# A state-space convolution and a gated feed-forward layer: the first part's tasks in another order, and both early inverse units behind the last spectral product

## The chip, the cores and the metric

One core of one Trainium2 chip. TensorE (PE) does the matmuls, VectorE (DVE), ScalarE (ACT) and GpSimd (POOL) the elementwise work, and SyncE (SP) issues nearly all transfers. The metric is the device time of one execution in microseconds, the median of several runs.

## The reference

`x` is one sequence of 2048 tokens with 640 channels; `mod` gives shifts, scales and gates from a small vector `c`.

```python
h = layernorm(x) * (1 + ca) + sa
K = 2.0 * real(einsum("dn,dnl->dl", C, exp(A * dt * pos)))       # one filter of 2048 taps for each channel
y = irfft(rfft(h, 2 * L) * rfft(K, 2 * L), 2 * L)[:L]            # a causal convolution
x = x + ga * (y + h * D_skip)
h = layernorm(x) * (1 + cb) + sb
x = x + gb * ((silu(h @ w1) * (h @ w3)) @ w2)                    # 640 -> 1728 -> 640
```

## The kernel before

The kernel has two parts. The **first part** (up to about 390 us) does the convolution through a Fourier transform written as matmuls, in five channel blocks `b` = 0 to 4 of 128 channels. The **second part** is the feed-forward layer, token block by token block; the change doesn't touch its code.

The first part is cut into 1532 *tasks*. Each is added to a plan with a name, an engine (or a choice of engines) and the tasks that it must follow. `Plan.run` then issues them in a fixed order, a list of numbers `ORDER` at the head of the file; a letter behind a number (a, d, p) picks ACT, DVE or POOL where a task may run on several. The class `InOrder` ties every instruction of an engine behind the one issued before it on that engine, so `ORDER` is at once the order of work on each engine. What an instruction needs from other engines it waits for; what stands behind it on its own engine waits too. For block `b`:

- `g{b}.{c}`, c = 0 to 7: the filter's generator, 16 channels at a time. `ph` and `z0` to `z2` on POOL (phases, magnitudes), `s0` to `s4` on ACT (sines), `m0` to `m4` on DVE (products), `p` on PE (`kps`), `r` on ACT and `d` on DVE (rows of the filter, `ks`). Ahead of them stand the tables `t{b}` and the exponentials (`al8{b}`, `exp{b}`, `mag{b}`; `al8` and `mag` on POOL or DVE).
- `h{b}.{i}`: the normalized input; `n` on ACT or DVE, `x` and `a` on DVE, stored by `o`, fetched back transposed by `h{b}.f`.
- `hh{b}.{i}` and `k{b}.{i}`, eight each: first transform stage of the input and of the filter. `m` on PE (`ps`), `e` the eviction to `sp` on ACT or DVE.
- `w{b}.{i}`, eight: second stage and spectral product. `f` on PE (`fh`) and `h` on ACT (`hq`) for the input, `k` on PE (`fk`) for the filter, `x0`, `x1`, `c` on DVE (`fp`, `fk`, `fp`). `k` needs all eight `k{b}.e`.
- `z{b}.{j}`, four: inverse of the second stage. `z` on PE (`fz`, two banks; `z{b}.{j}` takes the products w 2j and 2j + 1), `v0`, `v1` the copies to SBUF on ACT or DVE (`zt`, three buffers in turn; the last one `ztl`), `o0`, `o1` the stores on SP.

When the generator of block 4 is done, `change` closes its buffers, opens the buffers of the next part in their place, and issues on SP the loads of the first tokens (`low<-in_x`, four) and of a table (`low<-in_t_wd`). `fx` is a task without an instruction that stands for these loads in the plan. `fw0` and `fw1` load the first two weight tiles of the feed-forward layer (`wr`, `w2r`), `fa0`, `fa1` round them on ACT (`wh`, two instructions, and `w2h`), `fs0`, `fs1` take the rest on POOL. `change`'s x loads and `fw` are held until PE has done what was last issued to it at that place of the order (`behind`).

The last stage of the inverse for the first 512 tokens comes in two **units**, `ir0` and `ir1`: PE multiplies what `iz0` and `iz1` have read back for channel blocks 0 to 3 (`iy`, two banks in each unit), DVE adds it to x (`low`) and takes four statistics (`bn_stats`) for each of its two rows. The remaining channel block 4 comes after the plan: SP and ACT read back the stores of `z4`, PE passes the time with dummy matmuls (`awake`, 8 and later 3, kept so that PE's clock stays up), and the same `inverse` runs on four rows (L555). Then follow the layer norm, the transposes (`tp`) and the first matmuls of the feed-forward layer (`gu`).

In PSUM the tasks share four banks of one size: three of the tag `f`, taken in turn, and one of tag `x`; of four requests through `pbank` the third takes `x`. `ir` takes `f` banks. Further weight loads of the second part stand behind the plan in the program, but are not tied to its order on SP and lie between its transfers.

Of the kernel before, what the change touches and what calls it, by code (L numbers as in the profile page):

```python
# [34 lines left out]
10 29 25 39 153 35 26 13 62 154 60 155 47 72 74 70 76 66 89 27 48 5 93 87 91 98 49 36 100 33 95 50 94 34 51 32 88 37 52 38  # L35
152p 40 92 156d 53 96 157 90 9 158 6 54 102 159 167 104 55 170 99 11 171 168 97 56 103 184 176 172 57 105 178 173 169 58 188
185 111 177 107 186 67 193 101 122 187 68 189 174 194 160 195 190 64 179 175 123 191 180 109 161 163d 65 181 192 201 113 318
114 115 110 197 182 112 183 303 117 202 340 205 118 108 203 210 341a 106 162 211 124 308 196 204 127 116 138 198 218 313 206
119 128 207 199 130 212 221 129 125 208 134 164 131 165 135 132 209 219 166 222 133 235 140 139 63 214 126 309a 200 220 75 73
77 69 71 213 342 427 228 343a 215 136 223 319a 236 142 141 224 430p 431 229 137 239 428 310 216 429 217 311 227 312 344 304a  # L40
238 244 225 305 237 240 230 345a 424p 241 144 245 143 306 242 320 307 226 432 247 425 252 433 321 231 322 314d 232 255 246 315
253 243 426d 254 256 248 269 233 262 257 249 261 258 234 316 346 272 250 263 259 317 251 270 347a 264 348 260 146 271 145 273
265 274 278 286 275 279 266 280 276 349d 323 287 267 281 277 290 288 268 282 291 350 295 289 292 283 296 441 297 293 147 351d
284 294 285 298 352 148 458 299 445 149 0 582 698d 446 300 447 442 353d 592 324 699 443 450 328 325d 461 583d 336 459 460 329d
577 584 334 444 451 337a 585 301 972p 335a 700d 586 326 462 452 302 330 434 578d 327a 331a 354 448 467 593a 332 437p 579 438
468 439 580 333a 435 856 594 338 355a 453 449 436 358 463 581 595 851 464 475 440 364 454 469 465 455 339d 596 466 470 356 456
476 479 457 362 471 357 477 484 480 472 363 359 492 481 485 360 473 482 365 495 496 361 366 478 379 487 493 380 486 494 367
483 501 497 373 701 488 852a 375 502 857d 489 374 509 498 381 853 587 490 858 499 510 854 513 1399 859 390 704p 504 705 706
391 860 503 855 511 491 474 518 500 376 514 702 505 515 526 377 506 382 378 507 512 383 588a 407 519 527 384 520 528 408 385
861 589 516 703 508 530 590 517 521 591 368 529 707 388a 386a 522 389 543 531 387 536 523 532 537 1400d 369a 392 544 597 524  # L50
862a 545 525 393 1140 535 546 371a 394 533 1401 398 547 372 395 534 1402 1130 560 539 396 553 413 552 397 538 708 414 1403 370
399 540 548 863 564 400 549 561 864 565 554 709 865 598 541 566 569 710 542 401 550 599d 608 1131a 562 555 602 563 570 609a
1132 711p 606 973 712 571 713 604 1133 603d 714 1134 612 607d 1141d 600 601d 866 605a 974p 1142 567 610 613d 1246p 1404 1143
409 611d 551 572 670 568 1144 715 410 867a 636 573 411 574 732 556 719 1135 637 868 557 575 412 671 736 869 630 718 558 1405d
870 720 664 716 721 653 726 717 631 1409 1406 665 647 733 654 725 1407 871 648 734 741 1136a 415 681 724 735 1408 742 616 559
416 737 1414 1137 617a 743 738 417 682 1138 739 418 1139 687 722 744 1410a 620 727 880 723 1411 1125 688 728 749 881a 618 1412
740 576 1413 1415d 621a 729 766 753 876 619a 754 745 1126a 872 1416 750 1417 746 752 873d 1418 877a 1127 624 770 767 760 755
614 1128 768 625a 775 1129 628 615a 758 751 776 626 629a 769 759 622 627d 771 975 882 756 623d 772 761 402 883a 777 773 976
978d 730 778 979 419 774 980 403a 779 747 977 404 757 405d 632 420a 731 748 406 762 783 981 421 649 633 634 780 650 800 787
638 635 781 788 782 651 422a 763 639 789 423 652 655 784 764 640 790 884 656 801 641 878 885a 802 657 792 874 879a 785 658 765  # L60
786 875a 793 642 795 804 803 794 886 645a 643d 791 646 666 810 644 887a 817 1145 796 805 910 667 806 811 797 911 809 921 668
807 820 669 821 938 818 922 812 808 904 819 798 813 822 672 799 905 826 834 823 827 814 673 939 927 828 824 835 674 815 659
825 829 982 928 838 675 839 662d 676 660a 830 663 836 840 661 816 843 983 844 841 944 679d 837 842 831 846 680 945 985p 1247
683 986 677d 987 845 678 689 984 684 847 894 989 685 988 892 690 686 848 691 895a 990 832 893d 896 849 992 993 692 897d 693
991 1248d 994 850 1006 999 995 1000 961 696d 694a 955 998 1009 697 996 695 833 962 890 1001 1007 997 1160 1010 1002 1008 956
1015 1011 1150 1161d 1023 1012 1017 1003 1016 1151a 1013 891d 1146 1024 1027 1018 1014 1156 1025 1147a 1019 1028 1148 1026
1032 1157a 1033 1029 1020 1040 1149d 1034 1030 902 1031 1035 888 1041 1044 1036 1152 1043 889a 1049 1045 898 903d 1042 1046
1051 900 1249 1153a 1050 1047 899d 1158 901a 1052 1048 906 1159a 1057 1053 1004 912 907 1021 1005 1022 908 1037 1252p 913 1061
1250 1054 909 1062 1058 1038 914 1063 923 1039 915 1060 1055 1154 1066 1064 1059 1056 924 916 1419 1155a 1068 1251 925 1067
1074 926 917a 1065 1069 918 940 919a 1075 1078 920 1070 1184 1079 941 1077 1071 1083 1080 942 1076 1178 1185 1085 1081 1091  # L70
943 1212 1179 1084 1072 946 1213 1073 1086 1082 1092 1195 1095 947 1096 929 1094 1087 1196 948 1097 1088 1093 930 949 1218
1098 1108 1102 1089 950 931 1219 1101 1109 932 1100 953a 1111 933 951a 1090 954 1103 1099 1110 952 1112 1104 1201 1253 934a
1117 1254 1113 935 1118 957 1202 1255 1256 1119 1114 963 958 936a 959 1105 1115 937 964 1263 1116 1164 960 1106 1121 1162
1165a 1120 1266 1267 1172 1163a 965 1264 1268 1122 1107 966 1173a 1269 1265 1272 967 1274 1123 1280 1270 1273 1124 1275 1271
1176 970a 1283 1170 968d 1284 971 1177d 1285 969 1174 1281 1276 1286 1291 1168 1282 1175a 1289 1287 1235 1259d 1297 1290 1169a
1171d 1277 1236 1292 1288 1166 1260 1301 1298 1293 1302 1229 1167d 1278 1300 1303 1306 1294 1279 1299 1230 1308 1424 1304 1314
1307 1295 1180 1425a 1296 1309 1305 1420 1181 1317 1318 1310 1197 1319 1315 1182 1421a 1434 1320 1198 1316 1183 1311 1321 1199
# [107 lines left out]
class K:  # L185
# [866 lines left out]
    def run(self):  # L1052
# [46 lines left out]
        b = NB - 1  # L1099
# [13 lines left out]
        add = plan.add  # L1113
# [5 lines left out]
        z = {}  # L1119
        W = self.W["tail"]  # L1120
# [649 lines left out]
```

## Time and profile before

| | |
|---|---|
| median of 3 runs | 971.52 us (971.05 to 973.86) |
| profiled execution | 970.77 us |
| its span, first to last instruction | 968.8 us |
| mean granted TensorE clock | 0.966 |
| busy in the span: PE, DVE, ACT, POOL | 860.8, 712.9, 517.0, 336.1 us |
| moved by DMA | 113.18 MB |

A row of the timeline reads: start in us, duration in us, engine, line, operation, what is written from what, shape of output and input, how many instructions are merged; in brackets the engine's idle time before it and what ended it. A row of the groups ends with the total busy time and the mean of one instruction in ns, then the idle time ahead of them. A row of the windows has the stretch, its length, and for each engine the busy time and the number of instructions, then PE's granted clock, the share of the DMA engines and GB/s. In the page's strips each digit is the busy share of a fortieth of the span in tenths. L146 is the line of `InOrder`, through which all of the first part is issued.

### The profile page before, as it was taken

To read this page: it belongs to the slowest core of one execution; us is meant where nothing else is said; L and a number is where in the kernel's file an instruction comes from. 1 tells how busy PE (TensorE), PEld (TensorE's weight loads), DVE (VectorE), ACT (ScalarE), POOL (GpSimd) and SP (SyncE) were. 2 spreads that over 40 slices of the span, in tenths; PEclk is the share of its full clock that TensorE was granted. 3 is DMA by queue.
4 is the path that set the end of the run, shared out by engine and by line. 5 is a ranking of instruction groups with operands and counts; after the bars stand their busy time and mean duration, and the time that the engine had idled before them with its cause. 6 is when DMAs were issued, how large, how long until landed. Compare 5 with 4: busy or idle time off the path is not lost.

```text
span 968.8 us, 20106 instructions
## 1 busy us (share of the span) xinstructions
PE 860.8 (89%) x8017; PEld 685.6 (71%) x8017; DVE 712.9 (74%) x1292; ACT 517.0 (53%) x874; POOL 336.1 (35%) x345
## 2 busy tenths in 40 slices
PE   2165767899999997899999999999999999999997
PEld 1033655787878773667778888888888888888875
DVE  7888999999999973657684365566467777765763
ACT  5878879979888830523143243345234444445331
POOL 2789998599999530100000000000213223300000
PEclk9585989999999998999999999999999999999999
DMA  9956526624140296987523353223131122122242
GB/s 241 236 175 213 119 59 169 161 68 111 37 99 25 72 276 184 233 203 189 136 82 91 100 148 111 82 82 109 28 82 55 55 54 55 42 82 90 85 152 82
DMA packets 122821, 113.18 MB, mean 117 GB/s; under 512 B 11752, under 2 KB 106472, under 8 KB 121320
## 3 DMA queue, kind: packets, MB, share of 16 engines
q1 hardware_dynamic: 121992, 110.99, 42.6%
q8 instruction: 63, 1.03, 0.5%
q10 hardware_dynamic: 736, 0.92, 0.3%
q14 instruction: 30, 0.25, 0.1%
HBM read 90.91 MB, written 20.97 MB: 115 GB/s over the span
## 4 chain that ended last, share of the span: by engine, by line
PE 66%; DVE 13%; DMA 7%; ACT 6%; issue 3%; POOL 3%; SPq 1%; DVEq 0%; ACTq 0%; POOLq 0%
PE acc L1024 17%; PE p L777 16%; PE gu L987 6%; PE gu L989 6%; PE gu L988 6%; DVE yy L146 3%; DMA xs<-in_x 3%; PE ps L146 2%; PE kps L146 2%; DVE fp L146 2%; ACT tr L146 2%; PE fz L146 2%; DVE xx L146 2%; PE iy L555 2%; DMA sp<-in_w_mod 1%
## 5 line engine op out<-in xcount | busy, mean ns | idle before, releaser
L987 PE MATMUL gu<-xh,wh 128*128 128x512 f32 x270 | 105.0, 394 | 0.9 <-ACT xh L569 0.7
L989 PE MATMUL gu<-xh,wl 128*128 128x512 f32 x270 | 105.4, 390 | 0.0
L988 PE MATMUL gu<-xl,wh 128*128 128x512 f32 x270 | 105.3, 390 | 0.0
L777 PE MATMUL p<-x,wch 128*128 128x512 f32 x312 | 92.7, 390 | 0.0
L796 POOL TENSOR_TENSOR ws<-wp 128x256 f32<-128x256 f32 x13 | 9.6, 739 | 229.8 <-DVE wcl L570 114.9
L146 POOL TENSOR_TENSOR yy<-e,e 128x512 f32<-128x512 f32 x80 | 87.1, 1103 | 3.0 <-PE kps L146 2.3
L146 POOL TENSOR_TENSOR ph<-p,p 128x1024 int32<-128x1024 int32 x40 | 78.5, 1964 | 16.1 <-ACT tr L146 15.7
L146 DVE TENSOR_TENSOR yy<-yy,tr 128x512 f32<-128x512 f32 (+1 forms) x80 | 75.1, 944 | 5.0 <-POOL yy L146 4.6
L681 ACT ACTIVATE wh<-wr 128x640 fp32r<-128x640 f32 x51 | 34.9, 731 | 63.3 <-PE gu L988 54.1
L146 PE MATMUL kps<-yy,xx 128*32 128x64 f32 x2560 | 49.7, 231 | 20.9 <-DVE xx L146 11.5
L777 PEld LDWEIGHTS p<-x,wch 128*128 128x128 f32 x312 | 58.3, 188 | 12.6 <-ACT s L812 0.4
L146 PEld LDWEIGHTS kps<-yy,xx 128*32 128x32 f32 x2560 | 43.4, 115 | 32.8 <-issue 17.0
L987 PEld LDWEIGHTS gu<-xh,wh 128*128 128x128 f32 x270 | 50.6, 188 | 11.7 <-ACT xh L569 1.0
L989 PEld LDWEIGHTS gu<-xh,wl 128*128 128x128 f32 x270 | 50.7, 188 | 11.1 <-DVE wl L690 0.4
L988 PEld LDWEIGHTS gu<-xl,wh 128*128 128x128 f32 x270 | 50.8, 188 | 10.4 <-DVE xl L570 0.2
L693 POOL MEMSET w2l<- 64x640 f32 x1 | 0.6, 633 | 163.7 <-PE acc L1024 163.7
L777 PE MATMUL p<-x,wcl 128*128 128x512 f32 x156 | 57.0, 390 | 0.0
L146 ACT ACTIVATE tr<-ph,hpi 128x512 f32<-128x512 f32 x80 | 54.6, 689 | 3.2 <-DVE yy L146 2.3
L146 DVE TENSOR_TENSOR xx<-tr,xx 128x512 f32<-128x512 f32 x80 | 54.3, 680 | 2.1 <-ACT tr L146 1.9
L814 DVE TENSOR_TENSOR s<-p,s 128x512 f32<-128x512 f32 x52 | 34.7, 682 | 26.9 <-ACT s L812 22.9
L146 PE MATMUL ps<-wk,ks 128*64 128x128 f32 x640 | 42.0, 285 | 13.7 <-DVE ks L146 9.6
L1000 ACT ACTIVATE th<-gu 128x512 f32<-128x512 f32 x26 | 15.5, 598 | 69.9 <-PE gu L989 69.8
(368 smaller groups left out, 2315.9 us busy)
## 6 DMA issues: line engine op xcount, KB each, us to landing
wr<-in_w SPq DMA_DIRECT2D x52, 320.0 KB, 3.8
zd<-zt SPq DMA_DIRECT2D x39, 256.0 KB, 2.7
w2r<-in_w SPq DMA_DIRECT2D x26, 320.0 KB, 3.2
wp<-in_w SPq DMA_DIRECT2D x26, 320.0 KB, 3.5
wq<-in_w SPq DMA_DIRECT2D x26, 320.0 KB, 3.2
low<-zd SPq DMA_DIRECT2D x24, 320.0 KB, 5.9
xs<-in_x SPq DMA_DIRECT2D x16, 320.0 KB, 10.0
hs<-hb SPq DMA_DIRECT2D x20, 256.0 KB, 2.9
```

What stands on the lines that cost most here:

```text
L146: self.prev = self.k.order(f(*a, **kw), self.prev)
L555: mm = nc.tensor.matmul(py[pr * 64:(pr + 1) * 64, :n], self.wd[:, j0 + j, pr, :], z[pr][:, j, o:o + n], start=True, stop=True, tile_positi ...
L681: self.nc.scalar.activation(wh[:, i], raw[:, i], AF.Copy)
L693: self.nc.gpsimd.memset(w2l[64:].bitcast(F32), 0.0)
L777: nc.tensor.matmul(to, t[:, o], y[:, k], start=start and k == i == 0, stop=stop and (k, i) == (n - 1, 2), skip_group_check=True)
L796: G.tensor_tensor(s[0], a21, a22, op=ALU.add)
L814: add = lambda o, bk, s: V.tensor_tensor(o, bk, s, op=ALU.add)
L987: nc.tensor.matmul(pg, wh[:, k, :], xh[:, k, :], start=(k == 0), stop=False)
L988: nc.tensor.matmul(pg, wh[:, k, :], xl[:, k, :], start=False, stop=False)
L989: nc.tensor.matmul(pg, wl[:, k, :], xh[:, k, :], start=False, stop=(k == KT - 1))
L1000: nc.scalar.activation(th, gu[0], AF.Tanh, scale=0.5)
L1024: nc.tensor.matmul(acc[k], *two(a, w), start=(m == 0 and i == 0), stop=(m == 12 and i == 2))
```

## The change

One dependency of the units is replaced. Before, `ir0` and `ir1` could follow the evictions of the last block's first stage; now each must follow all four inverse transforms `z4.0.z` to `z4.3.z` of the last block:

```diff
         for u in range(2):
             add(f"iz{u}", "SP", 0, lambda u=u: load_z(u), ["change", "fx"] + [f"z{b - 1}.{j}.o{f}" for j in range(4) for f in range(2)], W, dma=[262144] * 4)
-            add(f"ir{u}", "PE", 2.4, lambda u=u: first_rows(u), [f"iz{u}"] + [f"{x}{b}.{i}.e" for x in ("hh", "k") for i in range(8)], W + 25)
+            add(f"ir{u}", "PE", 2.4, lambda u=u: first_rows(u), [f"iz{u}"] + [f"z{b}.{j}.z" for j in range(4)], W + 25)
```

And the whole list `ORDER` is another (its first and last lines):

```diff
-1 2 8 7 12 78 80 3 79 86 81 41 14 19 82 20 42 84 21 15 83 43 85 16 150p 44 17 4 22 151 18 23 28 61 45 59 30 120 31 46 121 24
...
-1513 1482a 1514 1483 1515 1498 1518d 1516a 1517 1519 1529 1499a 1500 1501a 1502
+1 2 12 10 8 78 80 9 79 3 86 81 42 14 20 41 84 13 19 15 82 43 85 21 83 16 22 150d 23 151 17 24 18 25 44 28 61 45 26 30 59 31 29
...
+1514 1515 1501d 1502 1529 1518d 1519 1516a 1517 1499a 1531 1500
```

No task is added or dropped. 59 of them change engine: 31 from ACT to DVE (10 of `k.e`, 8 of `hh.e`, 8 of `z.v`, 5 of `h.n`), 23 from DVE to ACT (7, 6, 5, 5), `al80`, `al81` and `mag0` from POOL to DVE, `mag2` and `mag4` from DVE to POOL.

The end of the order by engine, from the last generator product on. Before:

```
PE    g4.7.p k4.2.m k4.3.m k4.5.m k4.7.m k4.6.m z3.2.z k4.4.m k4.0.m k4.1.m w4.4.f w4.0.k w4.1.k w4.5.f
      w4.2.k w4.3.k z4.0.z w4.4.k w4.5.k z4.1.z w4.6.k w4.7.k ir1 z4.3.z z4.2.z ir0
ACT   g4.7.r k4.3.e k4.5.e k4.7.e k4.6.e z3.2.v1 k4.1.e w4.4.h w4.5.h fa0 z4.0.v0 fa1 z4.1.v1 z4.1.v0
      z4.3.v0 z4.2.v0 z4.2.v1
DVE   ... w4.5.c w4.6.x0 w4.6.x1 w4.7.x0 w4.6.c (ir1) w4.7.x1 w4.7.c z4.3.v1 (ir0)
SP    z3.3.o0 z3.3.o1 (change) fw0 z3.2.o1 z3.2.o0 fw1 iz1 z4.0.o0 z4.0.o1 iz0 z4.1.o1 z4.1.o0 z4.3.o0
      z4.3.o1 z4.2.o0 z4.2.o1
```

After:

```
PE    g4.7.p w3.5.k k4.6.m k4.7.m k4.4.m k4.1.m k4.3.m z3.2.z k4.0.m k4.2.m w4.5.f k4.5.m w4.4.f w4.1.k
      w4.0.k w4.2.k w4.3.k z4.0.z w4.4.k w4.5.k z4.1.z w4.6.k w4.7.k z4.2.z z4.3.z ir0 ir1
ACT   g4.7.r k4.6.e k4.7.e fa0 k4.0.e w4.5.h k4.5.e w4.4.h fa1 z4.0.v1 z4.1.v1 z4.1.v0 z4.3.v0 z4.2.v0
DVE   ... w4.6.x0 w4.6.x1 w4.6.c w4.7.x0 w4.7.x1 w4.7.c z4.2.v1 (ir0) z4.3.v1 (ir1)
SP    z3.3.o1 z3.3.o0 (change) fw0 fw1 z3.2.o0 z3.2.o1 iz0 z4.0.o1 z4.0.o0 iz1 z4.1.o1 z4.1.o0 z4.2.o1
      z4.3.o1 z4.3.o0 z4.2.o0
```

`change` stands behind k4.3.m's place on PE before, and behind w3.5.k after. In the list `fx` stood ahead of `fw0` before and stands behind it after.

More of the change, by code (lines that the diff above doesn't have):

```diff
@@ L38 @@
[L38 to L53, printed above, removed]
@@ new lines @@
+195 181 193 127 161 191 113 162 130 205 196 106 134 204 131 132 108 202 128 133 163d 203 182 210 192 140 139 183 206 164 211
+218 112 197 207 212 198 129 119 208 199 221 213 209 110 219 200 214 135 222 220 340 125 142 223 224 63 342 225 165 71 75 77 69
+73 341a 166 427 141 343a 215 228 126 314a 235 304d 144 143 216 136 309a 236 217 315 137 310 237 316 227 317 428 344 229 239
+429 230 146 240 145 241 244 238 245 226 424d 242 345a 252 247 425 246 311 430p 231 431 312 432 305 232 306 433 307 319d 256
@@ new lines @@
+508 384 517 527 520 391 407 597 1141a 521 543 522 1401 530 523 866 528 1142 408 531 535 529 524 536 532 525 544 1402 547 537
+1403 385 533 545 552 548 538 862a 546 553 703 554 534 1143 1414 707 388a 386d 560 549 413 539 389 863 368 550 1144 387 864 414
+708 564 555 865 551 600 371a 1415d 565 540 372 711p 601a 712 369a 556 713 541 370 1416 566 392 561 542 1417 602 393 563 1418
+569 398 603a 562 394 604 571 715 973 395 557 399 605d 612 709 400 718 570 598 613d 710 401 606 867d 599a 716 714 558 567 608
@@ new lines @@
+812 808 938 922 818 798 669 904 822 820 799 826 939 927 823 813 819 828 672 905 834 928 827 814 673 824 674 659 825 835 829
+838 815 836 830 944 839 843 982 660a 831 844 840 661 662d 945 675 663 841 816 837 676 832 846 842 985p 1247 983 845 683 833
+986 847 989 677d 689 684 678 848 685 990 690 892 686 1006 849 691 679a 893d 993 680 894 692 992 850 955 991 895a 998 902 994
+1007 956 1000 888 995 999 1248p 693 903a 889d 996 1009 1010 1001 1008 997 896 694a 1002 1023 890 1011 695 897d 696a 1003 1015
@@ new lines @@
+1268 1174 1264 965 1284 1269 966 1164 1266 1272 1123 967 1175d 1281 1165a 1274 1265 1289 1235 1124 970a 968d 1282 1273 971
+1176 1236 969 1257 1290 1270 1168 1283 1177a 1275 1271 1162 1258 1169a 1276 1170 1285 1163d 1297 1286 1277 1291 1171d 1287
+1166 1288 1259d 1298 1292 1229 1167a 1301 1299 1293 1180 1278 1306 1230 1300 1294 1302 1307 1181 1303 1260 1420 1308 1314 1295
+1182 1304 1432 1279 1421a 1296 1183 1305 1197 1317 1309 1318 1433a 1424 1315 1310 1319 1198 1261 1430 1320 1323 1316 1262 1199
@@ new lines @@
+1425a 1434 1325 1431a 1331 1321 1324 1311 1435a 1200 1322 1326 1186 1312 1334 1335 1313 1327 1203 1336 1332 1187 1337 1328
+1342 1333 1340 1338 1426 1204 1348 1329 1188 1422 1427a 1205 1189 1351 1423a 1341 1428 1349 1206 1352 1343 1339 1207 1350 1344
+1365 1353 1429d 1354 1345 1357 1358 1210a 1190 1366 1359 1346 1211 1369 1347 1208d 1355 1368 1374 1209 1370 1469 1360 1191a
+1367 1371 1231 1192 1376 1470 1475 1375 1193a 1232 1356 1194 1458 1330 1233 1476 1382 1361 1372 1237 1234 1459 1362 1373 1377
@@ new lines @@
+1386 1503 1238 1383 1363 1387 1378 1452 1504 1384 1239 1388 1379 1391 1385 1240 1453 1509 1392 1380 1389 1393 1241 1510 1394
+1390 1364 1395 1214 1244d 1242d 1396 1245 1215 1243 1220 1381 1216 1397 1398 1217 1520 1522 1448 1221 1450 1521 1449a 1222
+1444 1223 1451a 1438 1445d 1442 1525 1439d 1224 1443d 1523 1436 1225d 1227d 1440 1226 1437a 1524 1492 1228 1441d 1446 1493
+1486 1447a 1460 1487 1454 1471 1455 1461 1477 1456 1462 1457 1463 1472 1464 1473 1478 1526 1474 1479 1527 1480 1528 1488 1467a
@@ L88 @@
+1465d 1494 1468 1489 1466 1530 1490 1481 1495 1491 1496 1484a 1505 1497 1485 1506 1511 1507 1508 1482a 1512 1483 1498 1513
+1514 1515 1501d 1502 1529 1518d 1519 1516a 1517 1499a 1531 1500
 """
```

63 lines of the change are left out of this document (27 added, 36 removed).

## The prediction, made before the change was run

> **What bounds the kernel now.** I read the page first, then the windows of the first part, then the timeline of its end.
>
> ```profile
> span 968.8 us, 20106 instructions
> ...
> PE   2165767899999997899999999999999999999997
> ```
>
> The execution took 970.77 us, 1.97 more than its span; the median of the three runs is 971.52. From the 17th slice of 24.2 us on (about 390 us) PE is full to the end: that is the feed-forward part, which the change doesn't touch. The diff deals out only what comes before, so every microsecond won or lost there moves the end by as much.
>
> ```profile
> core 0: us, PE busy (x) PEld busy (x) DVE busy (x) ACT busy (x) POOL busy (x), PEclk, DMA share, GB/s
> 0.00:120.00 120.00, 56.71 (x905) 37.99 (x907) 100.63 (x200) 93.05 (x175) 89.72 (x103) 0.79 0.74 197
> 120.00:336.00 216.00, 192.71 (x4176) 162.26 (x4172) 211.28 (x383) 187.29 (x328) 187.49 (x180) 0.98 0.35 90
> ```
>
> VectorE (DVE) bounds the **head**: from 120 to 336 us it idles 216.00 - 211.28 = 4.7 us, before 120 us 19.4. What is dealt to it more must be paid unless those 19.4 us shrink. The **tail**, from the last generator product (end of the matmul group at 334.79, I call it G = 335.96) to the first feed-forward matmul, is another matter:
>
> ```profile
> 334.79 1.17 PE L146 MATMUL kps<-yy,xx 128*32 128x64 f32 x64
> ...
> 335.89 1.97 PE L146 MATMUL ps<-wk,ks 128*64 128x128 f32 x32
> ...
> 337.94 1.75 SPq L146 DMA_DIRECT2D low<-in_x  x4
> ...
> 340.90 0.95 SPq L146 DMA_DIRECT2D wr<-in_w  x2
> ...
> 347.18 2.01 PE L146 MATMUL fk<-sp,wb 128*64 128x128 f32 x32
> ...
> 348.31 0.69 DVE L146 TENSOR_TENSOR fp<-fk,hq 128x512 f32<-128x512 f32 x1 [2.01 <-PE fk L146]
> ...
> 350.66 1.50 ACT L146 ACTIVATE wh<-wr 128x640 fp32r<-128x640 f32 x2
> ...
> 352.24 0.74 ACT L146 ACTIVATE w2h<-w2r 128x640 fp32r<-128x640 f32 x1
> ...
> 356.69 1.99 PE L146 MATMUL fz<-fp,wz 64*128 64x512 f32 x8
> ...
> 361.37 1.14 PE L146 MATMUL iy<-low 128*64 128x512 f32 x4
> ...
> 362.21 0.74 DVE L146 TENSOR_TENSOR fp<-fp,fk 128x256 f32<-128x256 f32 x2
> ...
> 364.71 0.60 ACT L146 ACTIVATE zt<-fz 128x512 f32<-128x512 f32 x1 [5.38 <-DMA zd<-zt]
> ...
> 365.36 1.08 PE L146 MATMUL iy<-low 128*64 128x512 f32 x4 [2.85 <-ACT zt L146]
> ...
> 367.09 1.63 DVE L146 BATCH_NORM_STATS2 st_n<-low 128x6 f32<-128x128 f32 x8
> ...
> 368.64 0.68 DVE L146 TENSOR_TENSOR fk<-fk,hq 128x512 f32<-128x512 f32 x1
> ...
> 369.36 0.75 DVE L146 TENSOR_TENSOR fp<-fp,fk 128x256 f32<-128x256 f32 x2
> ...
> 369.92 5.29 PE L146 MATMUL fz<-fp,wz 64*128 64x512 f32 x16 [3.48 <-DVE fp L146]
> ...
> 375.14 1.94 PE L146 MATMUL iy<-low 128*64 128x512 f32 x8
> ...
> 375.28 1.08 ACT L146 ACTIVATE zt<-fz 128x512 f32<-128x512 f32 x2 [1.17 <-PE fz L146]
> ...
> 376.29 1.52 DVE L146 TENSOR_TENSOR low<-iy,low 128x512 f32<-128x512 f32 x2 [2.04 <-PE iy L146]
> ...
> 377.87 7.13 PE L146 MATMUL awake<-low,ident 128*128 128x512 f32 x16 [0.79 <-DVE low L146]
> ...
> 384.93 1.15 PE L555 MATMUL iy<-low 128*64 128x128 f32 x12
> ```
>
> Read it from the bottom. The last inverse (`iy` at L555, 384.93) starts when the dummy matmuls `awake` are through; these start at 377.87, when the adds of `ir0` are done. Higher up is the stall that the change is about: `ir1` (the `iy` at 361.37) stands on PE and DVE ahead of the last spectral product. Its second half waits for a PSUM bank until 365.36, and behind its adds and statistics the product w4.7 goes on only at 368.64, though DVE had been free of products since 362.21 + 0.74 = 362.95.
>
> **The change part by part: the tail.** (a) *Both inverse units last.* w4.7's two remaining steps follow at 362.95 instead of 368.64: -5.7 us. After them PE does one inverse transform (1.99) and not two (5.29): the other, z4.2, needs only w4.4 and w4.5. But the two units now stand where nothing hides them. By the new order ACT copies z4.3, then z4.2 (1.08 for both); `ir0`'s first bank is the one that z4.2's copy frees (the three f banks go in turn: z4.2's two tiles, z4.3's second, then `ir0`'s first). Then `ir0` runs until its second add (375.14 to 377.87 in the trace: 2.7), its eight statistics (1.63) and only behind them, on DVE, the last copy z4.3.v1 (0.69 like the product above), which frees `ir1`'s bank; `ir1` takes 2.7 again before `awake` may start. From the end of w4.7 to `awake`: 2.1 + 1.1 + 2.7 + 1.6 + 0.7 + 2.7 + 0.3 for the handing over = 11.2 us, against 377.87 - 370.11 = 7.8 now: **+3.4**. The last stores wait for that copy too (SP takes z4.3.o1, z4.3.o0, z4.2.o0 in this order), but `awake` covers them: from the end of the last copies now (376.36) to the last inverse stores, landing and reading back take 384.93 - 376.36 = 8.6 us, and behind the new last copy stand 0.1 + 2.7 + 7.1 = 9.9.
>
> (b) *The first weights.* The new order puts `fw0` ahead of `fx`, but `fx` issues nothing: the four x loads and the table's load behind them are issued inside `change`, ahead of `fw0` in both orders.
>
> ```profile
> L146 SPq DMA_DIRECT2D wr<-in_w x1: 384/384/384, 340.9 to 340.9; - x1
> ...
> DMA to landing us min/median/max: 9.6/9.6/9.6
> ```
>
> So the first weight tile lands at 340.90 + 9.6 = 350.5, which is 12.6 us after the first x load, and its split `fa0` on ACT starts right then (350.66). Now `fa0` is moved on ACT ahead of k4.0.e. What stands behind it: k4.0.e, w4.5.h, k4.5.e, w4.4.h; and every w4 product of the kernel's half needs all eight k4 evictions. The x loads are now held behind w3.5.k, which follows the last generator product: G + 1.0. The weights then land at G + 13.6; `fa0` takes 350.66 to 352.98, so 2.3: G + 16; three ACT steps of 0.6 follow: w4.1.k starts at G + 17.7, and w4.0.k, which the first DVE product needs, ends 2.0 later: G + 19.7. Now that product is at 348.31, G + 12.35. Without the wait PE's own list (w3.5.k, eight k4 of 1.97/2, z3.2 of 1.99, two w4 of 1.0, half a microsecond for banks) would give G + 13.4 and G + 15.4. The eight products take 348.31 to 362.95 and 1.44 for the last two steps: 16.1 us. So w4.7 ends at G + 35.8; it ends now at 370.11 = G + 34.15: **+1.6**, the 5.7 of (a) already in it. With (a), the tail is **+5.0** us; without the wait on the load it would be +0.7. Nothing excludes some more: the four-deep chain of zt buffers and stores (5.38 above) may bite again; I allow 2.
>
> A rule bears on this wait:
>
> ```profile
> 368.00:372.00 4.00, 2.08 (x6) 1.14 (x8) 2.07 (x7) 0.00 (x0) 0.00 (x0) 0.50 1.15 320
> ```
>
> The granted clock was 0.50 here after PE had stood nearly still, and 16 `fz` took 5.29 us where 8 take 1.99. The Trainium skill ("TensorE: Matmul & The Clock Gate", Part 1) says that an idle window of about 3.4 us halves the clock until PE has been busy as long. The trace agrees. By that rule PE's new idle of some 4 us (G + 13.4 to 17.7) would cost a third more on the first four w4 products, some 1.3 us: the sum would be 974.3 by it. I leave it out of the sum, as the four microseconds are themselves an estimate.
>
> **The head.** 59 tasks change engine; the rest of the new order is close to the old. Counting what stands ahead of the last generator chunk on DVE: 21 evictions come, 16 go, one product moves behind it; al80, al81 and mag0 come from POOL, mag2 and mag4 go there; five h normalizations come and five go.
>
> ```profile
> L146 DVE COPY sp<-ps 128x512 f32<-128x512 f32 x29 | 19.6, 681 | 1.6 <-PE ps L146 1.6
> ...
> L146 DVE TENSOR_TENSOR al<-al,j 128x1024 f32<-128x1024 f32 x1 | 1.4, 1415 | 0.0
> ...
> L146 DVE TENSOR_TENSOR e<-e,mag 128x512 f32<-128x512 f32 x3 | 2.9, 957 | 0.0
> ...
> L146 POOL TENSOR_TENSOR al<-al,j 128x1024 f32<-128x1024 f32 x2 | 3.9, 1957 | 0.0
> ...
> L146 DVE TENSOR_TENSOR yy<-yy,tr 128x1024 f32<-128x1024 f32 (+1 forms) x14 | 13.2, 946 | 4.6 <-POOL yy L146 4.6
> ...
> L146 DVE TENSOR_TENSOR xx<-tr,xx 128x512 f32<-128x512 f32 x13 | 8.9, 682 | 1.9 <-ACT tr L146 1.9
> ...
> 9.10 2.50 POOL L146 TENSOR_TENSOR ks<-al,j 128x1024 f32<-128x1024 f32 x1 [6.86 <-ACT al L146]
> ...
> 9.71 2.04 DVE L146 TENSOR_TENSOR xb<-e 128x128 f32<-128x128 f32 x1
> ...
> 27.16 0.29 DVE L146 TENSOR_TENSOR xb<-e 128x128 f32<-128x128 f32 x1
> ...
> 33.86 14.13 DMA xs<-in_x
> ```
>
> (The fifth and sixth row are from 60 to 120 us alone, the last from the chain.) Added work: 4 x 0.68 + 2 x 1.42 - 0.96 = **+4.6 us** on the engine that bounds the head. Against it: POOL is rid of 2 x 1.96 = 3.9 us (al80, al81) ahead of the second block, so the 4.6 + 1.9 us that DVE waited for POOL and ACT between 60 and 120 us can go; and the 128x128 subtraction that took 2.04 us beside POOL's al80, for 0.29 elsewhere, gets 1.75 back. That is 4.6 - 8.3 = -3.7. Bounds: +4.6, if no wait goes; -10, if all of the 19.4 us go but the 4.7 at the start that wait for loads. Against the lower end speaks that the fourth group's statistics, now moved ahead of most of the first chunk on DVE, can't start before its load lands at 33.86 + 14.13 = 48.0. I take **-3.5**.
>
> Sum: -3.5 + 5.0 = +1.5 us: 972.3 for the profiled execution, **973.0** for the median.
>
> **Rivals.** *DVE's added work is paid (slower).* If POOL and ACT weren't what held DVE before 120 us but only came last, other waits take their place. It decides from a head gain under 2.1 us, since 5.0 - 2.1 is 0.3%. With half of the 8.3 recovered the head is +0.5 and the time 977; with none it is 981. For it: DVE idles 2% after 120 us, so any stall of the new order comes on top. Against it: the extra work lies in the first block, where DVE idles 16%.
>
> *ACT isn't held (faster).* If the weights land earlier, or k4.0 comes late anyway, the tail is +0.7 and the time 968.7, on the edge of what can be told; with a head of -6 it is 966.2. For it: the 12.6 us are one sample. Against it: the same six loads go out in the same order on the same queue, and z3.3's two stores, moved to just ahead of them, can only make it longer.
>
> *The change doesn't do what it says*: the stall isn't removed but stands behind the last product. That is the +3.4, in the forecast.
>
> **How the numbers follow.** About 0.3% (2.9 us) is what a measurement of this kernel can tell from no change. Forecast, within that: 0.42. Slower: 0.33. Faster: 0.25. The range adds head -10 to +4.6 and tail +0.7 to +7 with their ends unlikely together: 965.5 to 979.
>
> **What would show it.** In the changed profile: DVE has no gap between w4.6 and w4.7; ACT's `wh` sits ahead of two `sp` evictions and an `hq`, with an idle ended by DMA or nothing, some 14 us after the last `kps`; the first `fp` product comes 19 to 20 us after the last `kps` (12.35 now); `awake` starts at about G + 47 (G + 41.9 now); the last `kps` ends near 332.5. I am wrong if that end comes later than 336, or if the first `fp` follows within 16 us.

## The result, and the profile after

| | before | after |
|---|---|---|
| median | 971.58 us (971.05 to 973.86, 4 runs) | 985.22 us (983.5 to 986.64, 4 runs) |
| profiled execution, span | 970.77, 968.8 us | 986.21, 984.4 us |
| G, end of the last `kps` | 335.96 | 345.49 |
| G to `awake` | 41.91 | 47.04 |
| `awake` to the first `gu` | 17.17 | 17.84 |
| first `gu` to the end of the last matmul | 567.43 | 567.74 |

After is slower: the ratio is 1.0131, with a 95% interval of 1.0107 to 1.0155. The four stretches account for it: 9.5 + 5.1 + 0.7 + 0.3 = 15.6 us between the two profiled executions. The tail is 5.1 us longer, as forecast. The head is 9.5 us longer where 3.5 less was forecast.

The windows of after, the second one up to G:

```profile
0.00:120.00 120.00, 55.97 (x843) 36.98 (x843) 100.97 (x198) 85.93 (x161) 77.20 (x90) 0.82 0.69 192
120.00:345.50 225.50, 199.41 (x4218) 167.23 (x4220) 217.48 (x391) 193.98 (x337) 195.34 (x192) 0.98 0.34 87
```

DVE (third pair) has 318.4 us of work up to G, 6.5 more than the 311.9 of before, and idles 27.0 us, 2.9 more. In the first 120 us it idles 19.0, as before (19.4). What it waits for there is another thing. The view of its waits up to 120 us (total, times, longest), before and then after:

```profile
DVE yy L146 <- POOL yy L146: 5.9, 5, 2.5
...
DVE xx L146 <- ACT tr L146: 1.9, 3, 0.9
...
DVE cols L146 <- PE pv L146: 1.0, 1, 1.0
```

```profile
DVE xx L146 <- ACT tr L146: 3.2, 1, 3.2
...
DVE cols L146 <- PE pv L146: 2.4, 1, 2.4
...
DVE ks L146 <- ACT ks L146: 2.0, 1, 2.0
DVE yy L146 <- ACT tr L146: 1.9, 3, 1.3
```

The wait for POOL is gone, as forecast. ACT's sines, the filter's rows and a column of PE have taken its place, to the same sum.

The timeline of after's end, beside the one in the prediction:

```profile
344.32 1.17 PE L146 MATMUL kps<-yy,xx 128*32 128x64 f32 x64
...
346.71 2.09 SPq L146 DMA_DIRECT2D low<-in_x  x4
...
349.32 1.11 SPq L146 DMA_DIRECT2D wr<-in_w  x2
...
351.55 7.44 SPq L146 DMA_DIRECT2D wr<-in_w  x2
...
359.82 0.74 ACT L146 ACTIVATE wh<-wr 128x640 fp32r<-128x640 f32 x1 [10.87 <-DMA wr<-in_w]
...
362.22 0.58 ACT L146 ACTIVATE sp<-ps 128x512 f32<-128x512 f32 x1
...
362.86 1.97 PE L146 MATMUL fh<-sp,wb 128*64 128x128 f32 x16 [6.34 <-ACT sp L146]
...
364.62 5.39 PE L146 MATMUL fk<-sp,wb 128*64 128x128 f32 x64
...
368.22 1.29 DVE L146 TENSOR_TENSOR fp<-fk,hq 128x512 f32<-128x512 f32 x2 [12.75 <-PE fk L146]
...
383.57 0.75 DVE L146 TENSOR_TENSOR fp<-fp,fk 128x256 f32<-128x256 f32 x2
...
386.35 3.92 PE L146 MATMUL iy<-low 128*64 128x512 f32 x16
...
389.05 1.64 DVE L146 BATCH_NORM_STATS2 st_n<-low 128x6 f32<-128x128 f32 x8
...
390.60 0.67 DVE L146 COPY ztl<-fz 128x512 f32<-128x512 f32 x1
...
391.19 1.28 DVE L146 TENSOR_TENSOR low<-iy,low 128x512 f32<-128x512 f32 x2
...
392.53 7.13 PE L146 MATMUL awake<-low,ident 128*128 128x512 f32 x16 [2.26 <-DVE low L146]
```

ACT waits 10.87 us for the first weight tile, and its evictions stand behind; PE stands still for 6.34 us, and DVE for 12.75. The first product comes at G + 22.7 (12.35 before), the last one ends at 384.32 = G + 38.8 (34.15 before). The stall between w4.6 and w4.7 is gone; both units run behind w4.7.

### The profile page after: what moved, and what is told of

Read it like the earlier page. It is cut to its first block, busy times and chain, and to the rows that moved or that the text cites. A ratio compares the mean times of both kernels' runs of the same rounds, so it can differ in the third digit from the quotient of the medians.

```text
span 984.4 us, 20092 instructions
## 1 busy us (share of the span) xinstructions
PE 868.9 (88%) x8017; PEld 692.3 (70%) x8017; DVE 722.2 (73%) x1301; ACT 514.5 (52%) x866; POOL 331.9 (34%) x344
## 4 chain that ended last, share of the span: by engine, by line
PE 69%; DVE 17%; ACT 5%; DMA 3%; issue 3%; POOL 2%; SPq 1%; DVEq 0%; ACTq 0%; POOLq 0%
PE acc L1024 17%; PE p L777 16%; PE gu L987 6%; PE gu L989 6%; PE gu L988 6%; DVE yy L146 3%; PE kps L146 3%; PE ps L146 3%; PE fz L146 3%; PE fh L146 2%; DVE fp L146 2%; PE fk L146 2%; PE iy L555 2%; DVE hn L146 1%; ACT tr L146 1%
## 5 line engine op out<-in xcount | busy, mean ns | idle before, releaser
L146 POOL TENSOR_TENSOR yy<-e,e 128x512 f32<-128x512 f32 x80 | 84.9, 1076 | 12.8 <-PE kps L146 10.8
L146 POOL TENSOR_TENSOR ph<-p,p 128x1024 int32<-128x1024 int32 x40 | 79.2, 1982 | 17.3 <-ACT tr L146 15.3
L146 DVE TENSOR_TENSOR yy<-yy,tr 128x512 f32<-128x512 f32 (+1 forms) x80 | 75.3, 944 | 3.2 <-ACT tr L146 2.6
L777 PEld LDWEIGHTS p<-x,wch 128*128 128x128 f32 x312 | 58.3, 188 | 12.6 <-ACT s L812 0.4
L146 PE MATMUL kps<-yy,xx 128*32 128x64 f32 x2560 | 51.2, 233 | 17.4 <-DVE xx L146 14.7
L146 PEld LDWEIGHTS kps<-yy,xx 128*32 128x32 f32 x2560 | 44.7, 116 | 30.4 <-POOL p L146 7.8
L146 PE MATMUL fh<-sp,wb 128*64 128x128 f32 x640 | 45.5, 288 | 18.9 <-ACT sp L146 6.3
L146 ACT ACTIVATE tr<-ph,hpi 128x512 f32<-128x512 f32 x80 | 54.9, 691 | 3.6 <-DVE yy L146 2.9
L146 DVE TENSOR_TENSOR xx<-tr,xx 128x512 f32<-128x512 f32 x80 | 54.1, 681 | 3.7 <-ACT tr L146 3.2
L146 PE MATMUL ps<-wk,ks 128*64 128x128 f32 x640 | 43.2, 288 | 14.6 <-DVE hb L146 9.9
L146 PEld LDWEIGHTS fh<-sp,wb 128*64 128x64 f32 x640 | 38.2, 140 | 25.1 <-ACT sp L146 6.6
```

Source lines behind the costliest of these rows:

```text
L146: self.prev = self.k.order(f(*a, **kw), self.prev)
L777: nc.tensor.matmul(to, t[:, o], y[:, k], start=start and k == i == 0, stop=stop and (k, i) == (n - 1, 2), skip_group_check=True)
```

## The experiments

The lists of tasks are mixed: "through X" means one order up to task X and then what is left of the other, each part on its own engines. The list of tasks is a line shorter in these kernels, so L146 is L145 below, and later lines are off by one in most of them. G, the first w4 product, the end of w4.7 and `awake` (these three from G on), `awake` to the first `gu`, and the first `gu` to the end of the last matmul are from the profiled execution; ratios are to runs of before on the same chip.

| run | ratio (95% interval) | G | first w4 | w4.7 ends | awake | to gu | rest |
|---|---|---|---|---|---|---|---|
| before | 1 | 335.96 | 12.35 | 34.15 | 41.91 | 17.17 | 567.43 |
| after | 1.0131 (1.0107 to 1.0155) | 345.49 | 22.73 | 38.84 | 47.04 | 17.84 | 567.74 |
| hb_ta | 1.0028 (1.0012 to 1.0045) | 336.46 | 21.84 | 37.94 | 45.54 | 18.38 | 567.04 |
| ha_tb | 1.0073 (1.0049 to 1.0097) | 344.51 | 12.28 | 33.26 | 40.81 | 18.67 | 566.96 |
| c0 | 1.0034 (1.0015 to 1.0054) | 339.22 | 12.36 | 34.03 | 41.89 | 19.30 | 566.46 |
| c1 | 1.0078 (1.0049 to 1.0107) | 341.38 | 12.36 | 33.97 | 41.24 | 18.19 | 567.82 |
| c2 | 1.0067 (1.0046 to 1.0088) | 342.84 | 12.35 | 34.61 | 42.60 | 18.52 | 567.95 |
| b0_a | 1.0102 (1.0075 to 1.0130) | 341.26 | 22.13 | 38.24 | 45.24 | 19.09 | 567.00 |
| c0_sine | 1.0007 (0.9991 to 1.0022) | 338.21 | 12.36 | 33.53 | 41.11 | 18.53 | 566.37 |
| b_pool | 0.9985 (0.9967 to 1.0002) | 336.60 | 12.37 | 33.52 | 40.97 | 17.59 | 568.52 |
| c1_pool | 1.0049 (1.0035 to 1.0062) | 340.14 | 12.36 | 34.02 | 41.38 | 19.31 | 566.52 |
| c1_evict | 1.0076 (1.0060 to 1.0092) | 344.00 | 12.35 | 34.14 | 42.13 | 18.24 | 567.60 |
| a_letters | 1.0265 (1.0233 to 1.0298) | 359.78 | 22.67 | 38.78 | 46.98 | 17.85 | 566.96 |
| b_ir | 0.9997 (0.9976 to 1.0017) | 337.38 | 12.36 | 28.40 | 42.45 | 18.77 | 566.07 |
| hb_hold | 1.0039 (1.0024 to 1.0055) | 336.30 | 13.84 | 29.94 | 44.56 | 18.36 | 568.27 |
| b_late | 1.0061 (1.0041 to 1.0081) | 336.35 | 12.36 | 31.60 | 39.22 | 17.18 | 576.31 |
| hb_hold_late | 1.0044 (1.0018 to 1.0070) | 334.79 | 13.80 | 29.90 | 38.43 | 18.10 | 575.41 |
| best1 | 1.0004 (0.9988 to 1.0019) | 335.72 | 13.82 | 30.42 | 39.30 | 21.04 | 566.98 |
| best2 | 1.0031 (1.0017 to 1.0045) | 335.80 | 13.80 | 29.90 | 38.83 | 18.62 | 573.54 |
| a_best | 1.0073 (1.0051 to 1.0095) | 344.22 | 13.83 | 29.93 | 39.51 | 19.95 | 569.01 |

The ratios come from 4 to 12 executions each, the other columns from a single one. Rows that share a part of the order show how far single executions lie apart: G is 334.8 to 337.4 in the eight that have all of before's head, 344.2 to 345.5 in the three that have all of after's; `awake` is 40.8 to 42.6 in the nine with before's tail, 45.2 to 47.0 in the four with after's. Differences smaller than this, 2 to 3 us, aren't read from one row.

### Head or tail

```diff
 hb_ta:  before through g4.7.m4
+        then what is left of after
 ha_tb:  after through g4.7.m4
+        then what is left of before
```

> The order of before up to the last generator products (g4.7.m4), and behind it what is left in the order of after. Theory A (the head carries 9.5 us of the loss, the tail 5): the last kps ends near 336, as before; the time is 971.5 + 5.1 (end of the last kps to awake, 47.0 us in after for 41.9 in before) + 0.7 (awake to the first gu) = 977.3. Rival (the tail is late only because the head is, and nothing is lost in it): 971.5 to 973.

> The order of after up to the last generator products (g4.7.m4), and behind it what is left in the order of before. Theory A: the last kps ends near 345, the tail is that of before: 971.5 + 9.5 = 981. Rival (head costs nothing by itself): 971.5 to 973.

Each half brings its own loss: G is at 336.5 and 344.5, `awake` at G + 45.5 and G + 40.8. Theory A holds as to where the loss is made. In time the halves are 0.28% and 0.73%, where after has 1.31%; hb_ta is 5.0 us longer by its span (973.8 for 968.8), but 1.2 to 4.4 by the timed runs, less than the 5.8 of theory A.

### The head: where

```diff
 c0:    after through g0.0.d,  then before
 c1:    after through g0.7.d,  then before
 c2:    after through g2.7.d,  then before
 b0_a:  before through g0.7.d, then after
```

> The order of after only through g0.0.d (the first filter chunk, which ends at 59.3 us in after for 54.3 in before), then what is left in the order of before. If the delay of the first chunk (ACT's normalization passes ahead of the first sines, DVE idle 3.2 us) is what stays: 4 to 6 us slower than before, as c1. If the later work of the first block is to blame (the reciprocal root, the transposed rows, the evictions dealt to DVE): within 2 us of before.

> The order of after through g0.7.d (the first block's filter, near 120 us), then what is left in the order of before. Theory C (the loss of the head is made in the first block, where after is 6.1 us late at g0.7.d, and stays): 5 to 7 us slower than before. Rival D (it is made in the later blocks): within 2 us of before.

> The order of after through g2.7.d (three of five blocks, near 245 us), then what is left in the order of before. By the lag at g2.7.d (4.0 us, and 2 to 5 at its neighbours): 4 us slower than before; theory C would give the 5 to 7 of c1 again, and rival D, with the loss in blocks 3 and 4 only, within 2 us of before.

> The order of before through g0.7.d (the first block's filter), then what is left in the order of after: the mirror of c1. Theory C (the head's loss is made in the first block): 5 to 8 us faster than after, so 977 to 980 where after has 985; the last kps ends 2 to 4 us later than in before. Rival D (made in the later blocks): 983 to 986.

G moves by +3.3, +5.4, +6.9 and, in ha_tb, +8.5 us as more of the new order is taken, but the last three steps are each within the scatter of single executions. In time c0 loses 0.34% (between its two forecasts), and c1, c2 and ha_tb lose 0.78, 0.67 and 0.73%, with intervals that overlap: the first block alone costs as much as the whole head, as theory C has it. The mirror contradicts theory C: b0_a has the first block of before, and G is still 5.3 us late, where 2 to 4 were expected; in time it loses 1.02%, against 0.28% of hb_ta, which has the same tail. So either part of the head loses when it is alone, and the losses of the parts don't add up to that of the whole.

### The head: the first sines

In the new order ACT does four passes over a group of x ahead of the first sines, and DVE waits for these:

```diff
 c0, ACT:  ... sq01
-sq12 sq10 sq13 sq11
 g0.0.s0 su23 g0.0.s1 su20 g0.0.s2
+sq12 sq10 sq13 sq11
```

> c0 (order of after through g0.0.d, then before) with one edit: the four normalization passes sq10 to sq13 go on ACT behind the first three sines g0.0.s0 to s2 instead of ahead of them. If the 3.2 us that DVE idles for the first sines are what c0 loses: the last kps comes back from G = 339.2 to 336 to 337, the time within 2 us of before. If not: G stays at 339 and another wait takes the place.

DVE's timeline in c0 and in c0_sine:

```profile
43.99 0.69 DVE L145 TENSOR_TENSOR xx<-tr,xx 128x512 f32<-128x512 f32 x1 [3.16 <-ACT tr L145]
```

```profile
42.02 0.69 DVE L145 TENSOR_TENSOR xx<-tr,xx 128x512 f32<-128x512 f32 x1 [1.55 <-ACT tr L145]
...
46.53 3.25 DVE L145 BATCH_NORM_STATS2 h_st<-xs 128x6 f32<-128x320 f32 x8 [2.03 <-DMA xs<-in_x]
```

The wait halves, and DVE then meets a load 2.03 us too early: the statistics of the fourth group stand early on DVE in this order, and they start at 46.5 us as in c0 (46.4), now by their load (the prediction put its landing at 48.0). Up to there nothing is gained. G comes back by 1.0 us of 3.3, less than expected and less than single executions differ; the time can't be told from before, and its interval overlaps c0's a little. The two timelines show that another wait took the place of the one that went; that the sines are part of the loss is likely by the time, but not shown.

### The head: the engines

```diff
 a_letters:  after, all 50 tasks of the head on the engines of before
 b_pool:     before, al80 al81 mag0 on DVE, mag2 mag4 on POOL, as in after
 c1_pool:    c1, al80 al81 mag0 back on POOL, mag2 on DVE
 c1_evict:   c1, nine evictions and normalizations back on their engines
```

> The order of after, but all 50 tasks ahead of the last generator products that changed engine go back to the engine of before (al80, al81, mag0 to POOL, mag2 and mag4 to DVE, evictions and normalizations as before). Theory A1 (the head loses by the work dealt to DVE: 5.4 to 6.6 us more of busy time at the last generator chunk): DVE's busy time falls by about 6 us and so does the end: 979. Rival A2 (it loses by the order itself, whatever engine runs the tasks): 984 to 986, DVE's idle time up by what its busy time falls.

> The order of before, with the engines of five tasks as in after: al80, al81 and mag0 on DVE, mag2 and mag4 on POOL. Theory P (the prediction's): POOL's relief takes away what DVE waited for POOL before 120 us (5.9 us) for 1.9 us more work: 3 to 4 us faster than before. Rival Q (another wait takes its place, the added work is paid): 1 to 3 us slower, DVE's idle time before 120 us unchanged near 19.

> c1 (order of after through g0.7.d, then before) with al80, al81 and mag0 back on POOL and mag2 on DVE. If the tables dealt to DVE are what c1 pays (DVE busy 316.3 us up to the last kps for 311.9 in before): DVE's busy time falls by 2 to 4 us and the last kps comes 2 to 4 us earlier than in c1, near 338 to 339. If not (as b_pool, where they made no difference): within 1 us of c1's 341.4.

> c1 with the nine evictions and normalizations of its part (h0.0.n, h0.2.n, h0.3.n, h1.0.n, k0.3.e, k0.4.e, hh0.3.e, hh0.4.e, hh0.5.e) on the engine that they had in before. If these are what c1 pays: DVE's busy time falls by 2 to 3 us and the last kps comes at 338.5 to 339.5 for 341.4 in c1. If the order binds engines (as a_letters, where putting the engines back made it 14 us slower): later than c1.

None gives back what the sum of durations says. a_letters is 14 us later at G than after: DVE's idle time grows from 27.0 to 40.6 us, and its busy time stays (319.2 for 318.4). Theory A1 (979) falls by it, and rival A2's 984 to 986 is 14 to 16 us short of the 1000 measured. c1_evict gives nothing back: its time is that of c1, and G is 2.6 us later. b_pool, the prediction's own step done alone, makes no difference that the interval shows, neither its 3 to 4 us nor a loss. DVE's wait for POOL in its first 120 us:

```profile
DVE yy L145 <- POOL yy L145: 2.8, 4, 1.0
```

It has halved, from 5.9, and DVE idles 18.6 us there for 19.4: most of what the one wait lost, the others took up. In c1_pool DVE's busy time is 316.3 us as in c1, though 2.4 us of tables have gone; other instructions became longer (the three `xb<-e` subtractions on 128x128 take 2.6 us for 0.9). Its 1.2 us at G are less than single executions differ, and the intervals of the two runs overlap. Putting engines back in a fixed order won nothing that is clear of the scatter, and in a_letters it cost much; that the added work as such costs the head its time isn't shown.

### The tail: what is behind the stall

```diff
 b_ir, PE:  z4.1.z w4.6.k w4.7.k
-ir1
 z4.3.z z4.2.z
+ir1
 ir0
```

> The order of before with one task moved: ir1 stands just ahead of ir0, behind z4.2.z; engines as before. Theory T (the idea of the change is right by itself): the stall of 5.7 us between the last products goes, w4.7 ends near 364.5, awake starts when the readback for ir0 has landed (370.8) and its adds are done: 373.5 to 374.5 for 377.87 in before, time 967 to 968. Rival (both units behind the last product cost as much as the stall): 971 to 974.

The stall goes to the tenth: w4.7 ends 5.75 us earlier. `awake` is no earlier, and the time is that of before, as the rival had it, though not for its reason. The timeline of b_ir:

```profile
365.59 6.01 PE L145 MATMUL fz<-fp,wz 64*128 64x512 f32 x16 [2.60 <-DVE fp L145]
...
365.89 0.60 ACT L145 ACTIVATE zt<-fz 128x512 f32<-128x512 f32 x1 [5.12 <-DMA zd<-zt]
...
374.92 0.60 ACT L145 ACTIVATE zt<-fz 128x512 f32<-128x512 f32 x1 [5.26 <-DMA zd<-zt]
...
376.34 3.56 PE L145 MATMUL iy<-low 128*64 128x512 f32 x8 [2.86 <-ACT zt L145]
```

Twice a copy waits over 5 us for a store, because `zt` has three buffers; the second time the unit's PSUM bank waits with it.

```diff
 hb_hold = hb_ta with, on ACT:
-k4.7.e fa0 k4.0.e w4.5.h k4.5.e w4.4.h fa1 z4.0.v1
+k4.7.e k4.0.e w4.5.h k4.5.e w4.4.h fa0 fa1 z4.0.v1
```

> hb_ta with one thing moved: fa0 and fs0 (splitting the first weight tile) go back behind z4.0.z, so that on ACT fa0 no longer stands ahead of k4.0.e, w4.5.h, k4.5.e and w4.4.h. Theory H (the tail of after loses by this hold on ACT, and its two units behind the last product gain): the first fp product falls from 21.8 us behind the end of the last kps (hb_ta) to 13 to 14, w4.7 ends at G + 29.5, awake starts at G + 37 to 38 for 45.5 in hb_ta and 41.9 in before: 3 to 5 us faster than before, 7 to 8 faster than hb_ta. Rival (something else in the tail, the loads or the stores on SP, holds the products as long): within 2 us of hb_ta.

Theory H's first half came as expected: first product at G + 13.8, w4.7 at G + 29.9, 8.0 us earlier than in hb_ta. `awake` gains 1.0 of them, where 7 to 8 were expected, and the time is no better than hb_ta's (0.39% for 0.28%), as the rival said. The timeline of hb_hold:

```profile
348.07 3.86 PE L145 MATMUL fk<-sp,wb 128*64 128x128 f32 x64
...
363.62 1.60 SPq L145 DMA_DIRECT2D zd<-zt  x2
...
369.12 0.60 ACT L145 ACTIVATE zt<-fz 128x512 f32<-128x512 f32 x1 [7.49 <-DMA zd<-zt]
369.77 5.68 PE L145 MATMUL fz<-fp,wz 64*128 64x512 f32 x14 [5.20 <-ACT zt L145]
```

Again a copy waits for a store (7.49), and PE waits for the copy. z4.0's stores are issued at 363.62 though the second copy ended at 358.4: on SP the third and fourth weight tile went out between. So the transfers, and no longer the products, seem to bound the tail; the next two runs test it.

### The tail: its transfers

```diff
-        dma = (nc.gpsimd if ahead and POOLQ else nc.sync).dma_start
+        start = (nc.gpsimd if ahead and POOLQ else nc.sync).dma_start
+        dma = lambda *x: self.held_back(start(*x)) if late else start(*x)
...
         self.load_x2(1)
+        for i in (2, 3):
+            self.ahead[0, i] = self.weights_load(0, self.ORDER[i], wp, late=True)
```

`held_back` ties a load behind the last inverse (POOLQ is False). b_late has this on before, hb_hold_late on hb_hold.

> The order of before; the loads of the third and fourth weight tile (six transfers, 1.9 MB, that lie between the inverse's stores and readbacks on SP) are held until the last inverse is done. Theory E (the tail is bounded by its transfers: what a shorter chain of products wins is lost to copies that wait for the stores): the copy that waits 5.4 us for a store goes on at once, awake starts 3.5 to 5 us earlier than 377.9, and the time falls by as much unless those two tiles now come too late. Rival F (the products bound the tail, transfers only fill): within 1 us of before.

> hb_hold with the same six transfers held until the last inverse is done. Theory E: the first fp product stays at G + 13.8 and w4.7 ends at G + 29.5 to 30, and now the copies of z4.1 no longer wait 7.5 us for a store: awake at G + 37 to 39 for 44.6 in hb_hold, 5 to 8 us faster than hb_hold and 3 to 5 faster than before. Rival F: within 2 us of hb_hold.

Theory E's point is met: `awake` is at G + 39.2 and G + 38.4, where products alone had not moved it. More than that is lost further on: the last column grows by 9 and 8 us. The view of PE's waits behind 385 us in hb_hold_late:

```profile
PE acc L1024 <- ACT w2h L682: 6.7, 1, 6.7
```

That is the fifth tile's splitting, whose load now comes behind others. Three runs try to keep the gain:

```diff
 best1, a_best (on hb_hold, and on after with the same hold undone):
+        self.nc = nc
         z = self.inverse_load(9728, 0, 4, cut, D, real.scalar)
+        for i in (2, 3):
+            self.ahead[0, i] = self.weights_load(0, self.ORDER[i], wp)
+        self.nc = real
 best2 (on hb_hold_late):
-            if b == 0 and m in (2, 4):
+            if b == 0 and m in (3, 5):
+                self.ahead[0, m + 1] = self.weights_load(0, self.ORDER[m + 1], wp)
                 self.load_x2(m // 2 + 1)
```

> hb_hold (order of before up to g4.7.m4, then that of after, fa0 and fs0 behind z4.0.z), and the six loads of the third and fourth weight tile tied on SP behind the last readback of the inverse, ahead of the next x loads. Theory E (the tail is bounded by its transfers; hb_hold_late and b_late lost their gain only because those two tiles came too late): awake again at G + 38 to 39, the first gu 3 to 4 us earlier than in before, and the time from the first gu to the end back at 567 to 568 us (575.4 in hb_hold_late): 3 to 4 us faster than before. Rival (the two tiles then hold up the readback or the next x loads as much): within 1.5 us of before.

> hb_hold_late (the loads of the third and fourth tile held until the last inverse is done) with the x loads of the third and fourth token block issued one step later, each behind the load of the next weight tile. In hb_hold_late the one wait that cost the gain is 6.7 us of PE on the splitting of the fifth tile, whose load stands behind eight x loads. Theory E with this order: awake at G + 38.4, first gu 3 to 4 us earlier than in before, that wait under 2 us, the time from the first gu to the end 568 to 571 us: 2 to 5 us faster than before. Rival (the transfers are the bound up to 430 us, whatever their order): the wait comes back elsewhere and the time is within 1.5 us of before or slower.

> The order of after as it is, but for the same two edits as in best1 (fa0 and fs0 behind z4.0.z, six loads behind the last readback). If head and tail add up, the head's 9.5 us stay and the tail gains 3 to 4 us on before: 5 to 7 us slower than before. If the late head hides the transfers (the tail of after has less to gain): 9 us or more slower.

best1 keeps the early `awake` (G + 39.3) and the short rest, and pays 3.9 us between: the tiles delay the last readback, and the transposes (`tp`) behind it are slower, at a granted clock of 0.62 from 390 to 394 us (1.00 in before from 391 to 395). The timeline of best1, and the transposes in before:

```profile
384.32 1.23 PE L554 MATMUL iy<-low 128*64 128x128 f32 x10 [1.37 <-DMA low<-zd]
...
390.83 4.07 PE L600 MATMUL tp<-ident,xn 128*128 128x128 f32 x20 [2.51 <-ACT xn L584]
```

```profile
391.90 2.40 PE L601 MATMUL tp<-ident,xn 128*128 128x128 f32 x20 [2.46 <-ACT xn L585]
```

best2 has the same wait for the fifth tile, of 5.4 us, in another order of the loads. The rival of both holds. A wait for transfers that is pushed off one place came up at the next in each of the four runs; none beats before. a_best takes 0.73% where after takes 1.31%: on the late head the two edits do help, by some 5.6 us.

## Why the prediction was wrong

*The head: -3.5 forecast, +9.5 measured.* This is the step that failed, in the term "recovered -8.3": nothing was recovered. DVE's idle time up to G didn't shrink by the 6.5 us of the two waits, it grew by 2.9. Of the term's three parts, the wait for POOL went (5.9 us to nothing in the first 120 us), those for ACT grew (all of them there from 4.5 to 8.1 us), and the idle time up to 120 us went from 19.4 to 19.0 us. The prediction read "what ended the idle time" as what caused it; b_pool, where POOL is relieved alone, shows the same thing. The third part, 1.75 us of slowed instructions, came back where it was looked for. These are the three subtractions in the groups of DVE up to G, before and after:

```profile
L146 DVE TENSOR_TENSOR xb<-e 128x128 f32<-128x128 f32 x3 | 2.6, 870 | 0.0
```

```profile
L146 DVE TENSOR_TENSOR xb<-e 128x128 f32<-128x128 f32 x3 | 0.9, 284 | 0.0
```

But other instructions that are the same in number became longer by more than that. The added work was nearly right: DVE has 6.5 us more for the 4.6 counted, and the rest is one more `zt` copy (0.7) and 1.2 net of such longer instructions. Together, 4.6 + 0.7 + 1.2 + 2.9 is the 9.4 to 9.5 us. This sum is an account, not the cause: the runs that put engines back don't give its terms back. What is shown is that the waits refilled and that c0, with the new order of the first chunk alone, already loses 0.34%. What makes the rest of the head's loss is open; no run here names it.

*The rivals.* "DVE's added work is paid" gave 981 with nothing recovered, and "any stall of the new order comes on top"; the result is that case, with such stalls (2.9 us) and the longer instructions (1.2) on top. Its reason ("other waits take their place") is what the waits show. Its chance was too small, and the range left the stalls out.

*The tail: +5.0 forecast, +5.1 measured*. That it agrees is luck: two errors of 3 us cancel.

- The wait on the first weights was seen rightly: the order on SP is as said, and ACT's `wh` comes 13.1 us behind the first x load (12.6 forecast), at G + 14.3 for 13.6. Its reach was not: the held evictions also hold a PSUM bank, so w4.4.f waits too and PE's list moves whole, 6.34 us idle. The first product came at G + 22.7 for 19.7.
- Part of that is the clock. The window 362 to 366 us of after (the columns are those of before):

```profile
362.00:366.00 4.00, 3.14 (x30) 3.15 (x32) 0.00 (x0) 2.90 (x7) 3.22 (x3) 0.50 0.70 197
```

  The 64 `fk` took 5.39 us at this clock; in hb_hold, where PE doesn't idle ahead of them, 3.86. By the rule of the Trainium skill ("TensorE: Matmul & The Clock Gate", Part 1) the prediction had estimated 1.3 us and left it out of the sum; the runs show 1.5. It belonged in the sum.
- From w4.7 to `awake` 11.2 were forecast and 8.2 measured: the units were priced one behind the other at 2.7 each, but `ir1`'s matmuls run during `ir0`'s statistics (one group of 16 from 386.35), so behind the copy only its adds are left (1.28). That the copy z4.3.v1 frees `ir1`'s bank was misread: these matmuls end at 390.27, and the copy starts at 390.60.
- "Without the wait it would be +0.7" was wrong: hb_hold measures +2.65. The "chain of zt buffers and stores", for which 2 us were allowed, is the tail's second bound. The gain of 5.7 from the stall is real at w4.7 (b_ir: 5.75) and never reaches `awake`.

*The other rivals.* "ACT isn't held" fell: it is held, for 10.87 us. "The change doesn't do what it says" was half true: the stall is removed, and both units then stand behind it, on the path to `awake`.

*The bounds for being wrong* were the right ones: the last `kps` ends later than 336.

## What to carry to other kernels

The releaser of a wait is the one that came last, which need not be the cause: before a wait is counted as won, look at when the next operand would have been there. In a stage that is bound by several things at nearly one time, price the second bound too (here the stores and loads of the stretch), since a shorter chain only moves the wait onto it. An order of tasks and its choice of engines belong together: here neither, changed or undone in part, gave what the sum of its durations said.

## What the hardware showed unexpectedly

A tiny DVE instruction can take as long as the POOL instruction beside it. The timeline of before, and that of after:

```profile
60.33 0.17 DVE L146 TENSOR_SCALAR rs_v_h<-h_ss 128x16 f32<-128x16 f32 x1
...
64.34 0.17 DVE L146 SCALAR_TENSOR_TENSOR rs_n_h<-h_nm,rs_y_h 128x16 f32<-128x16 f32 x1
```

```profile
65.07 1.28 POOL L146 TENSOR_TENSOR pB<-pB,e 128x512 int32<-128x512 int32 x1
65.08 1.30 DVE L146 TENSOR_SCALAR rs_v_h<-h_ss 128x16 f32<-128x16 f32 x1
...
69.52 1.95 POOL L146 TENSOR_TENSOR ph<-p,p 128x1024 int32<-128x1024 int32 x1
...
70.16 1.34 DVE L146 SCALAR_TENSOR_TENSOR rs_n_h<-h_nm,rs_y_h 128x16 f32<-128x16 f32 x1
```

Both DVE instructions work on 16 columns; in after they end within 0.03 us of POOL's. The Trainium skill has a reason ("SBUF — State Buffer", Who interferes with whom): the two engines share a pair of ports, and where both need it, whoever issues first has it for its whole instruction and the other is blocked. The trace agrees: in both pairs POOL's instruction starts first, and the DVE instruction ends with it. So DVE's busy time can hold waits of this kind, and c1_pool's equal busy time with less work is read so; that last point is argued, not measured apart.

SP's issue of a load isn't always short: the two `wr` loads at 351.55 held SP for 7.44 us in after, where the two at 349.32 took 1.11, and the stores behind them went out only at 360.62. What held SP, no run here shows.
